# A fused attention and two-layer kernel: half of the low parts of U leave VectorE, and the second pair's attention moves some slots on

## The chip, the cores and the metric

One Trainium2 core runs the whole program. The metric is the device time of one execution in microseconds (us). The engines are named as the profile names them: PE (TensorE, matmuls), PEld (its weight loads), DVE (VectorE), ACT (ScalarE), POOL (GpSimd) and SP, whose queue issues the DMAs.

## The reference, cut to what matters

```
a   = softmax of phi over the sequence                # per batch and head, 32 memories
k_m = a^T k ; v_m = a^T v                             # 32 x 64 each
att = softmax(q k_m^T / 8) over the memories          # 576 x 32 per head
x   = (att v_m) for 4 batches, 8 heads, 576 tokens    # 2304 x 512
h   = max(x w1, x w2, x w3)                           # 2304 x 768
y   = h w_out                                         # 2304 x 512
out = softplus(y w_in2) w_out2                        # 2304 x 2048, then 2304 x 512
```

The weights arrive as 64-bit floating-point numbers. Products are taken with each operand split into a high part (fp32r) and a low part (the rest), so every product is three matmuls: high x high, low x high, high x low.

## The kernel before

The four batches are worked in two pairs (576 x 2 = 1152 tokens each). A unit u is half of the heads of one batch; units 0 to 3 are the first pair, 4 to 7 the second. The stages are:

1. `PLAN`, a list written by hand: attention of units 0 to 3, the conversion of the weights of the first column blocks, the first U matrices and the first four `m1` steps.
2. `phase_a(0)`: 20 slots. In each slot stands one `m1`, and with some of them the U matrices of the next block. There are six column blocks i = 0 to 5 of 128 columns of w1, w2, w3.
3. `phase_o(0)`: 18 slots of `m1out` (the product with w_out).
4. `phase_a(1)` and `phase_o(1)`: the same for the second pair.
5. The last product pair (`m2in`, `m2out`, lines 850 and 882), which takes over half of the time and which the change doesn't touch.

Since attention is linear in v_m, the kernel doesn't form x. It forms U = v_m w (per block i and head pair p, `u_mm`), and multiplies U by the attention weights (`m1`). `u_mm` fills one PSUM bank `X` (128 x 384) by three matmuls (lines 561 to 563). The two halves of its partitions belong to the two batches of the pair. For each half, ACT writes the high part `uh` out of PSUM (line 568) and DVE subtracts it from `X` and writes the low part `ul` (line 572). The bank is free when the four instructions are done. `m1` uses three PSUM banks (18 matmuls at line 589), which ACT (line 593, `mt`) and DVE (lines 594, 596) empty into `h`. Six banks named `psm` serve both.

A weight tile is converted by the class `Conv`: ACT (line 259), DVE (lines 262 and 263), ACT for the high part (line 229), POOL for the low part (line 237). The tile `cg` in between has two buffers for all weights.

Next to its slots, a phase has a list `bg` of work that is put into the program behind slot n. Its numbers stand in the dictionary `C`: `att` (second pair: maxima of phi, exponentials, nothing, the products with k and v, their transposition), `wo` (conversion of w_out, three steps for each of six tiles), `load5` (loads of unit 5) and the literal 3 in `bg[3]` (loads of unit 4). Slots of 20 and over run behind `phase_a(0)`'s last. `C["hl"]` names the engine of the low part of h in `hsplit`.

The slots set the order of the program text. The order on each engine is laid down afterwards by the framework's planner, from times that it simulates (`schedule_with_timeline_sim=True`): an instruction that it holds to be ready may run ahead of others that stand before it. Tiles of one name share its buffers, and wait for each other there.

Of the kernel before, what the change touches and what calls it, by code (L numbers as in the profile page):

```python
# [9 lines left out]
F32 = mybir.dt.float32  # L10
F32R = mybir.dt.float32r
I32 = mybir.dt.int32
AF = mybir.ActivationFunctionType
ALU = mybir.AluOpType
# [117 lines left out]
]  # L132

C = {
    'load5': 5,
    'att': [[9, 9, 10, 11, 11], [10, 12, 12, 13, 13], [13, 13, 15, 15, 15], [15, 18, 19, 21, 21]],
    'wo': [[4, 5, 5], [6, 7, 7], [11, 11, 14], [11, 13, 17], [21, 22, 24], [23, 23, 23]],
    'scs': [[4, 4, 4, 4, 5, 6], [5, 5, 5, 6, 6, 7], [6, 6, 6, 7, 10, 10], [8, 11, 12, 13, 14, 18]],
    's1': ['pool', 'pool', 'pool', 'dve'],
    's2': ['dve', 'pool', 'pool', 'dve'],  # L140
# [2 lines left out]
    'w7': [4, 8, 9, 6],  # L143
    'w8l': 17,
    'wo_off': {(4, 0): 1, (5, 3): 0, (5, 1): -1, (3, 3): -1, (3, 0): 0, (4, 1): -2, (3, 2): 0, (5, 0): -1, (3, 1): 1, (5, 2): -2, (4, 3): 0, (4, 2): 0},
    'hl': ['dve'] + ['pool'] * 16 + ['dve'],
    'us0': 1,
    'us1': 0,
    'qpe': (0, 1, 2, 3),
# [3 lines left out]
def fused_kernel(ctx: ExitStack, tc: tile.TileContext, q, k, v, phi, w1, w2, w3, w_out, m_in, m_out, out):  # L153
# [7 lines left out]
    nc = tc.nc  # L161
# [4 lines left out]
    P = 128  # L166
    SCALE = 1.0 / float(D) ** 0.5
    NJ = FF1 // P
# [16 lines left out]
    def pool(stack, name, side=None, space=None):  # L185
        kw = {"side": side} if side else {"space": space}
        return stack.enter_context(tc.tile_pool(name=name, bufs=1, **kw))
# [6 lines left out]
    a_p = pool(a1_s, "a1", side="right")  # L194
# [7 lines left out]
    def psm():  # L202
        return ps_p.tile([P, 512], F32, tag="m", name="psm", bufs=6)
# [17 lines left out]
    for h in range(4):  # L221
        a = slice(32 * h, 32 * h + 32)
# [61 lines left out]
    def new_vT(pp):  # L284
        vT[pp] = tuple(a_p.tile([P, H, 64], F32R, tag=f"v{x}", name=f"v{x}", bufs=2) for x in "hl")

    def load_phi(u):
        b, g = units[u]
        hs = slice(4 * g, 4 * g + 4)
        if u == 2:  # L290
            ph = t_p.tile([P, 4, R4 + 1, M], F32, tag="qr", name="ph")
        else:
            ph = t_p.tile([P, 4, R4 + 1, M], F32, tag="ph", name="ph", bufs=2)
        dma(out=ph[:, :, 0:R4, :].rearrange("p h r m -> p h (r m)"),
                          in_=phi[b, hs, 0:R4 * P, :].rearrange("h (p r) m -> p h (r m)", r=R4))
        dma(out=ph[0:SREM, :, R4, :], in_=phi[b, hs, R4 * P:S, :].rearrange("h p m -> p h m"))
        nc.gpsimd.memset(ph[SREM:P, :, R4, :], 0.0)
        U[u]["ph"] = ph

    def load_x(u, i):  # L300
        b, g = units[u]
        hs = slice(4 * g, 4 * g + 4)
        src = (k, v)[i]
        if u in (2, 3):
            x = h_p.tile([P, 4, R4, D], F32, tag=f"h{2 * u - 1 - i}", name="kvm")
        else:
            x = t_p.tile([P, 4, R4, D], F32, tag=f"x{i}", name="kvm", bufs=2)
        if u in (2, 3):
            xr = wo_p.tile([SREM, 4, D], F32, tag=f"woh{2 * u - 2 + i}", name="kvr")
        else:  # L310
            xr = t_p.tile([SREM, 4, D], F32, tag=f"xr{i}", name="kvr", bufs=2)
        dma(out=x.rearrange("p h r d -> p h (r d)"),
                          in_=src[b, hs, 0:R4 * P, :].rearrange("h (p r) d -> p h (r d)", r=R4))
        dma(out=xr, in_=src[b, hs, R4 * P:S, :].rearrange("h p d -> p h d"))
        U[u]["x", i] = (x, xr)
# [234 lines left out]
    def u_mm(i, p, bls=(0, 1)):  # L550
        vh, vl = vT[i // NJ]
        vh_p = vh[:, 2 * p:2 * p + 2, :].rearrange("p a c -> p (a c)")
        vl_p = vl[:, 2 * p:2 * p + 2, :].rearrange("p a c -> p (a c)")
        hi, lo = wj_t[i, p]
        assert CK["w", 5 if i == 6 else i, p].done
        for bl in bls:
            for g in range(2):
                assert ("v", 2 * (i // NJ) + bl, g) in CK
            CK["u", i, p, bl] = 1
        X = psm()[:, 0:3 * P]  # L560
        nc.tensor.matmul(X, vh_p, hi, start=True, stop=False)
        nc.tensor.matmul(X, vl_p, hi, start=False, stop=False)
        nc.tensor.matmul(X, vh_p, lo, start=False, stop=True)
        halves = [(p % 2) ^ bl for bl in bls]
        for half in halves:
            uh, ul = Uj[i][(p % 2) ^ half]
            a = slice(64 * half, 64 * half + 64)
            nc.scalar.activation(out=uh[a, p // 2, :], in_=X[a], func=AF.Copy)
        for half in halves:
            uh, ul = Uj[i][(p % 2) ^ half]  # L570
            a = slice(64 * half, 64 * half + 64)
            nc.vector.tensor_tensor(out=ul[a, p // 2, :], in0=X[a], in1=uh[a, p // 2, :], op=ALU.subtract)  # L572

    def m1(i, bl, c):
        pp, j = i // NJ, jof(i)
# [78 lines left out]
    def phase_a(pp, bg, us):  # L654
# [16 lines left out]
        def u2(i, a):  # L671
            if a == 0:
                u_new(i)
            u_mm(i, a)
            u_mm(i, a + 1)
# [39 lines left out]
    for x in vT[0]:  # L715
        for s in range(4):
            nc.gpsimd.memset(x[:, 2 * s + 1 - s % 2].bitcast(F32), 0.0)
    STEPS = dict(ph=load_phi, ld=load_x, q=load_q, mx=att_max, ex=att_exp, ax=att_x, tr=att_tr, qT=att_q,
                 sc=att_sc, s0=att_sm0, s1=att_sm1, s2=att_sm2, fin=att_fin, wl=w_load, ca=conv_a, cb=conv_b,
                 un=u_new, u=u_mm, m1=m1)  # L720
    for st in PLAN:
        f = STEPS[st[0]]
# [7 lines left out]
    bg = defaultdict(list)  # L730
    def load_u(u):
        load_phi(u)
        load_x(u, 1)
        load_x(u, 0)

    bg[3].append(lambda: (new_vT(1), load_u(4)))
    bg[C["load5"]].append(lambda: load_u(5))
    for n in range(4):
        u = 4 + n
# [13 lines left out]
    bg = defaultdict(list)  # L753
# [63 lines left out]
    bg = defaultdict(list)  # L817
# [8 lines left out]
    bg = defaultdict(list)  # L826
# [75 lines left out]
    bg = defaultdict(list)  # L902
# [46 lines left out]
```

## Time and profile before

| | us |
|---|---|
| median of 3 runs (739.6 to 744.3) | 743.75 |
| profiled execution | 744.26 |
| its span in the trace | 742.5 |
| PE busy | 704.9 (95%) |
| DVE busy | 435.3 (59%) |
| ACT busy | 318.7 (43%) |
| POOL busy | 273.1 (37%) |

The span is what the trace shows of the profiled execution; 1.8 us lie around it. A busy share of PE is not PE at its peak: matmuls are pipelined, and a stretch of 100% can hold slower and faster streams.

### The profile page before, as it was taken

Reading aid. Unit: us, or ns where it says so; the run is one execution under the profiler, and the core shown is the slowest. Engines: PE = TensorE matmul, PEld = TensorE weight load, DVE = VectorE, ACT = ScalarE, POOL = GpSimd, SP = SyncE. Lnnn points to the kernel's source line nnn. Section 1 sums busy time; section 2 is a strip of 40 time slices with the busy share of each in tenths; the row PEclk is TensorE's granted clock in tenths of the full one; section 3 lists DMA queues with packets and bytes.
Section 4 is the critical chain, followed back from the end, with each engine's and each line's share of the span. In section 5 each row is a group of like instructions: output and inputs, shape, how many; then the busy total and the mean of one; then the engine's idle time right before and its main releaser. Section 6 shows DMA issues by size and latency. Waiting matters only on the chain. (4 is left out here: it accounts for less than half of the span.)

```text
span 742.5 us, 12551 instructions
## 1 busy us (share of the span) xinstructions
PE 704.9 (95%) x4784; PEld 630.4 (85%) x4784; DVE 435.3 (59%) x816; ACT 318.7 (43%) x662; POOL 273.1 (37%) x268
## 2 busy tenths in 40 slices
PE   4888899999979999989999999999999999999997
PEld 3656698999969999978998988989888989898896
DVE  5479888846969984683333486333794334433342
ACT  2466567644566753552333453222442223222221
POOL 2134333335765324662222353222642223322221
PEclk9989999999999999999999999999999999999999
DMA  8997633413224400440000132000231000011112
GB/s 240 256 305 216 199 100 116 123 56 100 80 71 135 129 2 30 141 143 28 0 1 1 29 113 86 1 0 1 84 115 29 1 1 0 1 43 43 42 43 85
DMA packets 55195, 59.26 MB, mean 80 GB/s; under 512 B 10080, under 2 KB 49504, under 8 KB 55136
## 3 DMA queue, kind: packets, MB, share of 16 engines
q1 hardware_dynamic: 55136, 58.47, 26.6%
q8 instruction: 37, 0.61, 0.4%
q14 instruction: 22, 0.18, 0.1%
HBM read 53.74 MB, written 4.72 MB: 79 GB/s over the span
## 5 line engine op out<-in xcount | busy, mean ns | idle before, releaser
L237 POOL TENSOR_TENSOR gl<-m,gh 128x384 fp32r<-128x384 f32 x96 | 100.6, 1049 | 255.1 <-ACT gh L229 238.1
L856 DVE TENSOR_SCALAR e<-pst 128x384 int32<-128x384 int32 x96 | 53.2, 555 | 135.8 <-PE pst L850 135.7
L858 ACT ACTIVATE L<-e 128x384 f32<-128x384 f32 x96 | 50.3, 524 | 186.1 <-DVE e L856 186.0
L882 PE MATMUL acc<-oh,gh 128*128 128x512 f32 x288 | 113.9, 395 | 0.4 <-ACT gh L229 0.4
L882 PE MATMUL acc<-ol,gh 128*128 128x512 f32 x288 | 113.5, 394 | 0.0
L850 PE MATMUL pst<-yb,ih 128*128 128x384 f32 x384 | 102.1, 336 | 0.0
L589 PE MATMUL psm<-ah,uh 128*128 128x288 f32 x288 | 87.2, 307 | 6.1 <-ACT ya L229 2.1
L860 DVE SCALAR_TENSOR_TENSOR m<-pst,L 128x384 f32<-128x384 f32 x96 | 53.4, 556 | 55.9 <-ACT L L858 55.9
L589 PE MATMUL psm<-al,uh 128*128 128x288 f32 x288 | 85.5, 298 | 0.0
L589 PE MATMUL psm<-ah,ul 128*128 128x288 f32 x288 | 83.8, 298 | 0.6 <-DVE ul L572 0.6
L882 PE MATMUL acc<-oh,gl 128*128 128x512 f32 x288 | 82.7, 394 | 0.0
L229 ACT ACTIVATE gh<-m 128x384 fp32r<-128x384 f32 x96 | 50.0, 523 | 63.1 <-DVE m L860 60.2
L237 POOL TENSOR_TENSOR wl<-cg,wh 128x384 fp32r<-128x384 f32 x44 | 46.3, 1058 | 74.9 <-ACT wh L229 61.0
L850 PEld LDWEIGHTS pst<-yb,ih 128*128 128x128 f32 x384 | 70.0, 188 | 3.4 <-DVE m L860 0.7
L262 DVE TENSOR_SCALAR cg<-cg 128x384 int32<-128x384 int32 (+2 forms) x88 | 46.8, 531 | 37.3 <-ACT cg L259 19.8
L850 PE MATMUL pst<-y0h,ih 128*128 128x384 f32 x192 | 65.5, 341 | 2.7 <-DVE m L860 2.6
L850 PE MATMUL pst<-y0l,ih 128*128 128x384 f32 x192 | 65.1, 339 | 0.0
L850 PE MATMUL pst<-y0h,il 128*128 128x384 f32 x192 | 65.0, 339 | 0.0
L850 PE MATMUL pst<-yb,il 128*128 128x384 f32 x192 | 64.4, 335 | 0.0
L589 PEld LDWEIGHTS psm<-ah,uh 128*128 128x128 f32 x288 | 53.9, 188 | 11.1 <-ACT ya L229 2.3
L882 PEld LDWEIGHTS acc<-oh,gl 128*128 128x128 f32 x288 | 53.6, 187 | 11.4
L882 PEld LDWEIGHTS acc<-oh,gh 128*128 128x128 f32 x288 | 54.1, 188 | 10.6 <-ACT gh L229 0.9
(134 smaller groups left out, 1419.4 us busy)
## 6 DMA issues: line engine op xcount, KB each, us to landing
wraw<-in_moe_w_dram SPq DMA_DIRECT2D x66, 256.0 KB, 3.7
raw<-in_moe_w_in_dram SPq DMA_DIRECT2D x16, 512.0 KB, 3.8
raw<-in_moe_w_out_dram SPq DMA_DIRECT2D x16, 512.0 KB, 3.7
out_dram<-o SPq DMA_DIRECT2D x18, 256.0 KB, 2.1
kvm<-in_v_dram SPq DMA_DIRECT2D x8, 512.0 KB, 6.2
kvm<-in_k_dram SPq DMA_DIRECT2D x8, 512.0 KB, 7.1
wor<-in_moe_w_out_dram SPq DMA_DIRECT2D x6, 512.0 KB, 4.4
qr<-in_q_dram SPq DMA_DIRECT2D x4, 576.0 KB, 4.1
```

What stands on the lines that cost most here:

```text
L229: nc.scalar.activation(out=dst, in_=src, func=AF.Copy)
L237: e.tensor_tensor(out=dst, in0=src, in1=hi, op=ALU.subtract)
L262: nc.vector.tensor_scalar(out=gi, in0=gi, scalar1=3, scalar2=None, op0=ALU.logical_shift_left)
L589: nc.tensor.matmul(x, l[:, t, ws], r[:, cs], start=(n == 0), stop=(n == 5))
L850: nc.tensor.matmul(hx, l[:, ds], r[:, cs], start=(n == 0), stop=(n == 3 * ND - 1))
L856: nc.vector.tensor_scalar(out=e.bitcast(I32), in0=hx.bitcast(I32), scalar1=0x7FFFFFFF, scalar2=None, op0=ALU.bitwise_and)
L858: nc.scalar.activation(out=L, in_=e, func=AF.Softplus, scale=-1.0)
L860: nc.vector.scalar_tensor_tensor(out=m, in0=hx, scalar=0.0, in1=L, op0=ALU.max, op1=ALU.add)
L882: nc.tensor.matmul(acc[0][t], l[:, t * P:(t + 1) * P], r, **kw)
```

## The change

Three things are changed. First, `att`, `wo`, `load5` and the loads of unit 4 stand later in `phase_a(0)`: unit 4's loads behind slot 7 instead of 3, unit 5's behind 9 instead of 5, unit 4's attention from slot 11 instead of 9, and the conversion of w_out spread evenly over slots 10 to 21 instead of 4 to 24. Second, for the blocks of the first pair (`i < NJ`), the low part of the upper half of the partitions is no longer made by DVE out of PSUM: ACT copies that half of `X` to a new tile `xc` in SBUF (one buffer), and POOL subtracts `uh` from it. The lower half and the second pair stay as they were. Third, the very first low part of h goes to POOL instead of DVE, in both `phase_o`.

```diff
-    'load5': 5,
-    'att': [[9, 9, 10, 11, 11], [10, 12, 12, 13, 13], [13, 13, 15, 15, 15], [15, 18, 19, 21, 21]],
-    'wo': [[4, 5, 5], [6, 7, 7], [11, 11, 14], [11, 13, 17], [21, 22, 24], [23, 23, 23]],
+    'load5': 9,
+    'att': [[11, 11, 12, 12, 13], [13, 13, 14, 14, 15], [15, 15, 16, 16, 17], [17, 18, 19, 20, 21]],
+    'wo': [[10, 11, 11], [12, 13, 13], [14, 15, 15], [16, 17, 17], [18, 19, 19], [20, 21, 21]],
...
-    'hl': ['dve'] + ['pool'] * 16 + ['dve'],
+    'hl': ['pool'] * 17 + ['dve'],
...
-            nc.vector.tensor_tensor(out=ul[a, p // 2, :], in0=X[a], in1=uh[a, p // 2, :], op=ALU.subtract)
+            if half and i < NJ:
+                xc = a_p.tile([P, 3 * P], F32, tag="xc", name="xc", bufs=1)
+                nc.scalar.activation(out=xc[a], in_=X[a], func=AF.Copy)
+                nc.gpsimd.tensor_tensor(out=ul[a, p // 2, :], in0=xc[a], in1=uh[a, p // 2, :], op=ALU.subtract)
+            else:
+                nc.vector.tensor_tensor(out=ul[a, p // 2, :], in0=X[a], in1=uh[a, p // 2, :], op=ALU.subtract)
...
-    bg[3].append(lambda: (new_vT(1), load_u(4)))
+    bg[7].append(lambda: (new_vT(1), load_u(4)))
     bg[C["load5"]].append(lambda: load_u(5))
```

## Rows read from the trace of the kernel before

**Rows 1.** Busy time by engine in stretches of the span (us, with instruction counts).
```profile
core 0: us, PE busy (x) PEld busy (x) DVE busy (x) ACT busy (x) POOL busy (x), PEclk, DMA share, GB/s
45.00:95.00 50.00, 45.02 (x558) 34.98 (x559) 45.65 (x100) 32.00 (x73) 18.09 (x17) 0.90 0.80 229
95.00:145.00 50.00, 50.00 (x443) 45.64 (x442) 42.37 (x98) 36.02 (x87) 17.44 (x19) 1.00 0.36 112
160.00:205.00 45.00, 44.79 (x257) 41.69 (x256) 34.54 (x59) 22.23 (x48) 28.69 (x27) 1.00 0.26 80
205.00:230.00 25.00, 19.68 (x117) 18.14 (x116) 18.07 (x32) 16.63 (x37) 18.68 (x17) 0.93 0.27 85
```

**Rows 2.** Waits of PE from 45 to 95 us: total, times, longest.
```profile
PE psm L398 <- ACT kvd L387: 2.5, 1, 2.5
PE psm L469 <- ACT qT L229: 1.9, 2, 1.5
PE psm L589 <- DVE ul L572: 1.2, 2, 0.6
PE psm L589 <- ACT ah L513: 1.1, 1, 1.1
```

**Rows 3.** PE in order of time: the step that starts the slots of phase_a(0).
```profile
89.49 1.15 PE L589 MATMUL psm<-ah,uh 128*128 128x288 f32 x6 [1.15 <-ACT ah L513]
```

**Rows 4.** DVE in order of time, 74 to 81 us: start, length, line, tiles.
```profile
74.27 2.17 DVE L572 TENSOR_TENSOR ul<-psm,uh 64x384 fp32r<-64x384 f32 x4
...
77.36 1.11 DVE L572 TENSOR_TENSOR ul<-psm,uh 64x384 fp32r<-64x384 f32 x2
78.51 0.97 DVE L237 TENSOR_TENSOR hlo<-h,hh 128x384 fp32r<-128x384 f32 x1
79.51 1.14 DVE L572 TENSOR_TENSOR ul<-psm,uh 64x384 fp32r<-64x384 f32 x2
80.58 0.73 DVE L498 TENSOR_REDUCE ssm<-sT 128x18 f32<-128x576 f32 x1
```

**Rows 5.** ACT in order of time, 71 to 77 us.
```profile
71.06 1.85 ACT L568 ACTIVATE uh<-psm 64x384 fp32r<-64x384 f32 x4
...
73.28 0.96 ACT L568 ACTIVATE uh<-psm 64x384 fp32r<-64x384 f32 x2
...
74.82 0.99 ACT L568 ACTIVATE uh<-psm 64x384 fp32r<-64x384 f32 x2
75.72 0.67 ACT L492 ACTIVATE sT<-sT 128x576 f32<-128x576 f32 x1
```

**Rows 6.** POOL at 71 us, and all its low parts of weights (ns: shortest, median, longest).
```profile
71.18 1.34 POOL L491 TENSOR_TENSOR sT<-sT,smx 128x576 f32<-128x576 f32 x1
...
L237 POOL TENSOR_TENSOR wl<-cg,wh x44: 997/1012/1521, 14.0 to 268.6; 128x384 fp32r<-128x384 f32 x44
```

**Rows 7.** Two DVE operations over the whole span (ns: shortest, median, longest).
```profile
L572 DVE TENSOR_TENSOR ul<-psm,uh x96: 482/552/562, 51.1 to 275.2; 64x384 fp32r<-64x384 f32 x96
L263 DVE SCALAR_TENSOR_TENSOR cg<-wraw,cg x44: 509/552/1401, 12.6 to 267.4; 128x384 int32<-128x384 int32 x44
```

**Rows 8.** SP's queue in order of time: the first load of q of unit 4.
```profile
50.22 0.79 SPq L200 DMA_DIRECT2D qr<-in_q_dram  x1
```

**Rows 9.** DVE by line, 45 to 95 us: busy us, mean ns, idle before.
```profile
L572 DVE TENSOR_TENSOR ul<-psm,uh 64x384 fp32r<-64x384 f32 x16 | 8.7, 552 | 0.2
...
L341 DVE TENSOR_TENSOR m<-ph 128x256 f32<-128x256 f32 x4 | 2.2, 552 | 0.2 <-DMA ph<-in_phi_dram 0.2
```

**Rows 10.** ACT by line, 95 to 145 us.
```profile
L568 ACT ACTIVATE uh<-psm 64x384 fp32r<-64x384 f32 x32 | 15.2, 483 | 1.4 <-PE psm L563 1.0
...
L259 ACT ACTIVATE cg<-wor 128x256 f32<-128x256 f32 x8 | 3.4, 436 | 5.6 <-DMA wor<-in_moe_w_out_dram 3.2 <-POOL wl L237 2.4
```

**Rows 11.** Waits of PE from 205 to 230 us.
```profile
PE psm L589 <- ACT ya L229: 2.1, 1, 2.1
PE psm L561 <- DVE ul L572: 1.4, 1, 1.4
```

## The prediction

> **What bounds the kernel now.** Read the busy time by stretches first, then PE's waits in the stretches that the change touches, and then the order on the engines ahead of the waits that remain.
>
> The change works between about 45 us (the first U matrices) and 230 us (the second pair's first slots). In between there are three kinds of stretch [rows 1]. From 45 to 95 us PE is busy 45.02 of 50 us, so 5.0 us are open, and DVE is busy 45.65 of 50, nearly all of the time. From 95 to 145 us PE is busy for all 50.00 us, and from 160 to 205 for 44.79 of 45: there the other engines have slack (DVE 42.37 of 50 and ACT 36.02 of 50 in the first of the two), and nothing that is made faster on them can shorten the time. From 205 to 230 us PE is busy 19.68 of 25; 5.3 us are open at the turn from the first pair to the second.
>
> So a gain can come from two places only, 5.0 us at the start and 5.3 us at the turn. At the start PE's waits are 2.5 us for a scaled k or v on ACT, 1.9 for a transposed q on ACT, 1.2 for the low parts of U on DVE and 1.1 for the attention weights `ah` [rows 2]. The last is the one that counts most, because it is the gate of the slots: the wait just ahead of 89.49 us is for the `ah` of unit 3, without which no `m1` of the pair's second batch can start [rows 3]. Ahead of it PE fills its time with products of the second pair, which have to be done anyway.
>
> What made unit 3 late is read off DVE and ACT. Its exponentials at 75.72 us stood behind eight copies `uh` of block 1 on ACT [rows 5], although GpSimd had given the input at 71.18 + 1.34 = 72.52 us [rows 6]. The sums of these exponentials (line 498) then started at 80.58 us instead of 76.4 (75.72 + 0.67), because eight low parts `ul` (2.17 + 1.11 + 1.14 us) and one `hlo` (0.97) were in front of them on DVE in the same seven microseconds [rows 4]. That is the queue from which the change takes instructions.
>
> **Low parts of U.** There are 6 blocks x 4 head pairs = 24 `u_mm` of the first pair, each with one upper half. So DVE loses 24 of its 48 `ul` at 0.552 us [rows 7], 13.2 us; ACT gets 24 copies and POOL 24 subtractions. The nearest row for the copy is the `uh` copy, the same shape out of PSUM: 483 ns [rows 10]. For the subtraction it is the low part of a weight, the same 384 elements a partition on twice the partitions: 997 to 1521 ns, median 1012 [rows 6]. From below, half of the partitions could cost half of that, 0.5 us; I take 1.0, since the shape along the free axis is the same, and keep 0.5 for the range.
>
> Of the 24, eight lie in the start (16 `ul` there, blocks 0 and 1 [rows 9]), 16 in the slots. In the slots PE waits for nothing, so the 16 x 0.552 = 8.8 us taken from DVE are worth nothing there. At the start the path is unit 3's. In front of line 498 DVE loses four `ul` (4 x 0.552 = 2.2 us) and the `hlo` (0.97, the third part of the change): 3.2 us, so that the sums could start at 77.4. But ACT gets four more copies in front of the exponentials: four copies in a row take 1.85 us [rows 5], so each further one adds (1.85 - 0.48) / 3 = 0.46, and four add 1.8 us, so that these end at 76.4 + 1.8 = 78.2. The later of the two counts: 78.2 against 80.58, a gain of 2.4 us.
>
> From that goes what GpSimd takes back from DVE. Beside GpSimd some operations of DVE with both inputs in SBUF are held up: line 263 takes 509 to 1401 ns, median 552 [rows 7], while `ul`, which reads PSUM, stays within 482 to 562. Five more POOL operations of 1.0 us fall in these seven microseconds (four subtractions and `hlo`). If none holds anything up the price is 0; if each holds one up by the full 1401 - 552 = 849 ns it is 4.2 us, and the gain is gone with 1.8 us to spare. The nearest row in kind is the median, which is at the undisturbed end; I take 0.12 us for each, 0.6 in all. The sum for the start is -2.4 + 0.6 = -1.8 us, with the bounds -5.0 (all of PE's open time) and +1.8.
>
> The Trainium skill speaks against this part (Perfetto Trace Analysis, Optimizing Scalar/DVE Operations): since GpSimd and DVE share an SBUF read port, moving work from the one to the other may not help. By that rule the start would give nothing back, and the sum would be 0. The trace agrees for line 263 (up to 1401 ns), but not for the operation that is moved, whose longest is 562 ns.
>
> In block 0 (48 to 58 us) the same edit puts four copies, 1.8 us, on ACT ahead of the q transposes of unit 2, for which PE waited 1.5 us [rows 2]. ACT idles behind them, so unit 2 can be up to 1.8 us later; unit 3's exponentials had 75.72 - 72.52 = 3.2 us of waiting on ACT, which cover that. I take 0. Without that cover it costs 1.8 us.
>
> **The slots of the second pair's attention and of w_out.** By name the work moves two slots and more. But the planner doesn't keep to the slots where an engine is idle in its own times: q of unit 4, which stands in the program behind all of `phase_a(0)`, is issued at 50.22 us [rows 8], and the maxima of phi (line 341) of all four units of the second pair, slots 9 to 15, run before 95 us [rows 9]. Moving them to slots 11 to 17 leaves them ready at the same times; nothing with a higher place in the program is ready instead. So SP's queue keeps its loads early (the load of w_out may come behind those of unit 5, not in front), and I cost the move at nothing. The cover for that is PE's 50.00 of 50 [rows 1]. For the conversion of w_out the cover is the same: its eight steps on ACT between 95 and 145 us (3.4 us [rows 10]) move to later slots, and `m1out` takes the tiles one by one, in order, over 45 us. If the cover is gone, the bound is from below the 5.0 us open at the start, and from above the 5.3 us of the turn once more.
>
> **What else a new wait holds up.** `xc` has one buffer, so a copy waits for the subtraction before, and everything behind it on ACT waits with it: `mt` and `uh` copies, which empty PSUM banks. A `u_mm` takes ACT 2 x 0.48 + 0.46 = 1.4 us and POOL 1.0 us, so alone the buffer is free in time. In the slots ACT goes from 36.02 to 36.02 + 16 x 0.46 = 43.4 of 50 us, 87%, less what w_out's later slots take away. I cost it at 0 there.
>
> **The sum.** The profiled execution took 744.26 us (a span of 742.5 and 1.8 around it). Less 1.8 us that is 742.5. It stands 0.5 us above the median of the runs, so against the median of 743.75 the change gives 741.95: 742 us. With the bounds of the start, -5.0 to +1.8, and block 0's 1.8 on top, this case spans 739 to 747.
>
> **The rivals.**
> *ScalarE becomes the bound (slower).* The planner puts another POOL operation, 1.0 us, between two subtractions. The next copy `xc` then stands on ACT for 1.0 us, in order, and `mt` behind it; `m1` can't get its three banks and PE stops. ACT's slack in the slots is 50 - 43.4 = 6.6 us. It decides from the seventh of the 16 copies that stands for a full operation; when all do, 16 x 1.0 - 6.6 = 9.4 us go to PE: 753, without the gain at the start. For it: ACT would be the most loaded engine beside PE. Against it: POOL is busy only 17.44 of 50 us there [rows 1], and 33 with the 16 subtractions. When half of the excess reaches PE it is 748.
> *The turn gets worse or better (either sign).* There PE waits 2.1 us for banks that ACT empties late and 1.4 for `ul` [rows 11]. If a later second pair comes to the turn with as much again to do, the 5.3 us open there double: 749. Against it: the last of unit 7's steps stays at slot 21.
> *The slots do work as written (faster).* If the second pair's 2.2 us of maxima and the rest of it leave the start, and the turn loses its waits too, all open time goes: 5.0 + 5.3 = 10.3 us, 733. Against it: rows 8, where the planner goes past twenty slots.
> *GpSimd takes back what DVE gives (no change).* Each of the five POOL operations ahead of unit 3's sums holds DVE up by 2.4 / 5 = 0.48 us, a little over half of the 0.85 that line 263 shows at its worst [rows 7]; the start gives nothing, and the time is 744. Against it: that line's median is only 0.04 us over its shortest. The skill's rule above leads to the same time.
>
> **How the numbers follow.** Differences under 1% (7.4 us) can hardly be told from no change here: three runs span 739.6 to 744.3. The forecast has 0.41, no change 0.14, ScalarE as bound 0.22, a worse turn 0.10, the faster case 0.13. Faster by over 1% means under 736.3: nearly all of the faster case and a little of the forecast, 0.14. Slower by over 1% means over 751.2: half of ScalarE's case, half of the turn's and some of a reordering that I can't see, 0.20. Within 1% is left with 0.66. The range goes from the fastest case's end, 733, to ScalarE's worst, 753; the forecast's own range is 739 to 747.
>
> **What would show it.** In the profile after, DVE should be 10 to 14 us less busy, ACT 11 and POOL 24 us more (12 if half of the partitions cost half). The first `m1` behind unit 3's `ah` should start near 87.7 us instead of 89.49, and everything up to 205 us should be earlier by the same. The maxima of the second pair should still run before 95 us. PE should show no waits from 95 to 145 us; waits there for `mt` would speak for ScalarE as the bound. The prediction is wrong if the planner's new order moves the turn at 205 us by more than the start gives, in either direction.

## The result, and the profile after

| | before | after |
|---|---|---|
| median (4 runs each) | 743.58 us | 752.0 us |
| range of the runs | 739.6 to 744.3 | 751.5 to 754.7 |
| profiled execution | 744.26 us | 754.73 us |
| span, mean granted clock | 742.5 us, 0.988 | 753.0 us, 0.979 |
| PE busy | 704.9 us | 708.5 us |
| DVE, ACT, POOL busy | 435.3, 318.7, 273.1 | 436.2, 330.4, 303.1 |

The ratio is 1.013, 95% interval 1.0104 to 1.0156: the changed kernel is slower by 9.7 us (1.3% of 743). The forecast was 742.

Busy time by stretches of the changed kernel, first the four of [rows 1], then the start in pieces of 5 us (columns as there):

```profile
45.00:95.00 50.00, 40.64 (x449) 31.30 (x449) 39.42 (x82) 33.23 (x73) 26.42 (x25) 0.83 0.75 216
95.00:145.00 50.00, 50.00 (x600) 42.45 (x600) 34.59 (x73) 36.86 (x85) 26.20 (x25) 1.00 0.30 92
160.00:205.00 45.00, 40.19 (x228) 37.51 (x227) 39.02 (x63) 20.60 (x46) 29.84 (x29) 0.96 0.28 88
205.00:230.00 25.00, 20.29 (x97) 19.36 (x96) 18.43 (x24) 14.43 (x33) 16.43 (x15) 0.86 0.35 108
75.00:80.00 5.00, 3.09 (x30) 2.24 (x29) 3.35 (x9) 4.87 (x12) 4.15 (x5) 0.97 0.01 2
80.00:85.00 5.00, 2.65 (x10) 2.06 (x10) 5.00 (x10) 3.55 (x9) 3.75 (x4) 0.50 0.34 107
85.00:90.00 5.00, 4.46 (x48) 3.92 (x47) 4.31 (x8) 2.61 (x6) 3.02 (x4) 0.84 0.59 169
```

The same pieces of the kernel before:

```profile
75.00:80.00 5.00, 3.85 (x37) 3.03 (x29) 4.89 (x11) 3.07 (x6) 1.20 (x2) 1.00 0.84 250
80.00:85.00 5.00, 4.88 (x62) 4.07 (x62) 4.97 (x15) 3.34 (x9) 1.00 (x1) 1.00 0.51 134
85.00:90.00 5.00, 3.85 (x113) 3.04 (x113) 4.87 (x12) 2.09 (x6) 3.72 (x3) 1.00 0.63 179
```

The start was to gain 1.8 us. Instead PE is busy 40.64 of 50 us from 45 to 95 us, 4.4 us less than in [rows 1], and from 80 to 85 us it is busy 2.65 of 5 us at half clock, with 10 matmuls where the kernel before ran 62. From 160 to 205 us PE has lost another 4.6 us. In between it is busy all the time, as forecast.

PE's waits from 45 to 95 us in the changed kernel (total, times, longest), beside [rows 2]:

```profile
PE psm L398 <- ACT kvd L387: 3.1, 1, 3.1
PE psm L469 <- ACT qT L229: 2.6, 1, 2.6
PE psm L594 <- ACT xc L574: 1.9, 1, 1.9
PE pst L350 <- DVE md L349: 1.4, 1, 1.4
PE psm L449 <- ACT xc L574: 1.1, 1, 1.1
PE psm L594 <- POOL ul L575: 1.0, 1, 1.0
```

`ah` of unit 3, the wait on which the prediction rested [rows 3], is gone. Two new names stand in its place: `xc` on ACT and `ul` on POOL (line 594 is `m1`, 574 the copy, 575 the subtraction). ACT and then POOL in order of time show where these two stood:

```profile
76.16 0.67 ACT L492 ACTIVATE sT<-sT 128x576 f32<-128x576 f32 x1
78.84 0.47 ACT L574 ACTIVATE xc<-psm 64x384 f32<-64x384 f32 x1
80.86 0.68 ACT L513 ACTIVATE ah<-aT 128x576 fp32r<-128x576 f32 x1
81.56 0.49 ACT L574 ACTIVATE xc<-psm 64x384 f32<-64x384 f32 x1
83.47 0.49 ACT L574 ACTIVATE xc<-psm 64x384 f32<-64x384 f32 x1 [0.34 <-POOL ul L575]
87.55 0.49 ACT L574 ACTIVATE xc<-psm 64x384 f32<-64x384 f32 x1
```

```profile
79.96 0.99 POOL L575 TENSOR_TENSOR ul<-xc,uh 64x384 fp32r<-64x384 f32 x1
82.12 1.31 POOL L575 TENSOR_TENSOR ul<-xc,uh 64x384 fp32r<-64x384 f32 x1 [1.17 <-ACT xc L574]
83.51 2.38 POOL L237 TENSOR_TENSOR wl<-cg,wh 128x384 fp32r<-128x384 f32 x2
85.97 1.00 POOL L575 TENSOR_TENSOR ul<-xc,uh 64x384 fp32r<-64x384 f32 x1
88.11 0.99 POOL L575 TENSOR_TENSOR ul<-xc,uh 64x384 fp32r<-64x384 f32 x1 [1.00 <-ACT xc L574]
```

Unit 3 did come earlier: its sums (line 498) start at 76.87 us against 80.58 [rows 4]. But block 1's four copies lie spread over 78.84 to 88.04 us, between other work of ACT, and the last low part of block 1 is finished on POOL at 89.10 us. In the kernel before DVE had finished all of them by 80.65 [rows 4]. The `m1` steps on block 1 need these low parts, and the PSUM banks that the copies hold. The gate moved from unit 3's `ah` to block 1's U. The fifth `h`, the first that needs unit 3's `ah`, was to come 1.8 us earlier; it is done at 97.5 us against 94.7 before.

DVE is not relieved either. Its rows by shape, changed kernel (busy us, mean ns), then the kernel before:

```profile
L577 DVE TENSOR_TENSOR ul<-psm,uh 64x384 fp32r<-64x384 f32 x72 | 39.0, 549 | 9.3 <-ACT uh L568 4.6 <-ACT xc L574 3.2 <-PE psm L594 0.9
L263 DVE SCALAR_TENSOR_TENSOR cg<-wraw,cg 128x384 int32<-128x384 int32 x44 | 34.5, 791 | 0.7
L263 DVE SCALAR_TENSOR_TENSOR cg<-wor,cg 128x256 int32<-128x256 int32 x12 | 10.0, 845 | 0.0
```

```profile
L572 DVE TENSOR_TENSOR ul<-psm,uh 64x384 fp32r<-64x384 f32 x96 | 52.2, 552 | 8.6 <-ACT uh L568 7.4
L263 DVE SCALAR_TENSOR_TENSOR cg<-wraw,cg 128x384 int32<-128x384 int32 x44 | 29.4, 673 | 0.5
L263 DVE SCALAR_TENSOR_TENSOR cg<-wor,cg 128x256 int32<-128x256 int32 x12 | 6.4, 544 | 0.0
```

`ul` went down by 13.2 us, as forecast; line 263, the same 56 instructions, went up by 8.7. The trace shows what these 8.7 us go with. Of the 44 operations on `wraw`, those that had POOL at work for half of their length or more were 13 before and 21 after, with medians of 1111 and 1243 ns; the others took a median of 549 and 552 ns.

### The profile page after: what moved, and what is told of

Read it like the earlier page. It is cut to its first block, busy times and chain, and to the rows that moved or that the text cites. A ratio compares the mean times of both kernels' runs of the same rounds, so it can differ in the third digit from the quotient of the medians.

```text
span 753.0 us, 12579 instructions
## 1 busy us (share of the span) xinstructions
PE 708.5 (94%) x4784; PEld 634.0 (84%) x4784; DVE 436.2 (58%) x790; ACT 330.4 (44%) x686; POOL 303.1 (40%) x294
## 5 line engine op out<-in xcount | busy, mean ns | idle before, releaser
L594 PE MATMUL psm<-ah,uh 128*128 128x288 f32 x288 | 89.0, 310 | 6.5 <-ACT mt L598 2.8
L262 DVE TENSOR_SCALAR cg<-cg 128x384 int32<-128x384 int32 (+2 forms) x88 | 48.8, 559 | 35.8 <-ACT cg L259 18.6
L237 POOL TENSOR_TENSOR wl<-cg,wh 128x384 fp32r<-128x384 f32 x44 | 48.0, 1098 | 43.7 <-ACT wh L229 41.0
L887 PEld LDWEIGHTS acc<-oh,gh 128*128 128x128 f32 x288 | 53.9, 187 | 10.5 <-ACT gh L229 0.9
```

Source lines behind the costliest of these rows:

```text
L237: e.tensor_tensor(out=dst, in0=src, in1=hi, op=ALU.subtract)
L262: nc.vector.tensor_scalar(out=gi, in0=gi, scalar1=3, scalar2=None, op0=ALU.logical_shift_left)
L594: nc.tensor.matmul(x, l[:, t, ws], r[:, cs], start=(n == 0), stop=(n == 5))
L887: nc.tensor.matmul(acc[0][t], l[:, t * P:(t + 1) * P], r, **kw)
```

## The experiments

The difference is the ratio to the kernel before on the same chip, less one, times 743 us. "Copies" are the `xc` copy on ACT and its subtraction on POOL.

| kernel | ratio, 95% interval | difference |
|---|---|---|
| the change | 1.013, 1.0104 to 1.0156 | +9.7 |
| e1: without the copies | 1.002, 0.9997 to 1.0042 | +1.5 |
| e2: copies alone, all blocks | 1.015, 1.0123 to 1.0177 | +11.1 |
| e3: the change, old w_out slots | 1.0167, 1.014 to 1.0194 | +12.4 |
| e4: the change, two buffers | 1.0113, 1.0083 to 1.0144 | +8.4 |
| e5: copies in blocks 0, 1 | 1.0055, 1.0034 to 1.0076 | +4.1 |
| e6: copies in blocks 2 to 5 | 0.9955, 0.9934 to 0.9976 | -3.3 |
| e7: copies, DVE subtracts | 1.0125, 1.0086 to 1.0164 | +9.3 |
| e8: copies that nobody reads | 1.0088, 1.006 to 1.0117 | +6.5 |
| e9: the change, copies in 2 to 5 | 1.0071, 1.0044 to 1.0098 | +5.3 |
| e10: copies in block 0 | 0.9991, 0.9972 to 1.0009 | -0.7 |
| e11: copies in block 1 | 1.0059, 1.0038 to 1.0081 | +4.4 |
| e12: copies in 0 and 2 to 5 | 1.0014, 0.9993 to 1.0034 | +1.0 |
| e13: copies in 1 to 5 | 1.0135, 1.0103 to 1.0167 | +10.0 |
| e15: e11 with filled stop | 1.001, 0.999 to 1.0029 | +0.7 |
| e16: the filling alone | 1.0012, 0.9988 to 1.0035 | +0.9 |
| e17: the change, filled stop | 1.0063, 1.0046 to 1.0081 | +4.7 |
| e18: e13, all `ya` on ACT | 1.0094, 1.0074 to 1.0113 | +7.0 |

### Which of the three parts

e1 is the changed kernel with line 572 as before (the slots and the engine of `h` stay changed); e2 is the kernel before with the copies alone; e3 is the changed kernel with the old `wo`.

```diff
 e1 (to the changed kernel)
-            if half and i < NJ:
...
+            nc.vector.tensor_tensor(out=ul[a, p // 2, :], in0=X[a], in1=uh[a, p // 2, :], op=ALU.subtract)
 e3 (to the changed kernel)
-    'wo': [[10, 11, 11], [12, 13, 13], [14, 15, 15], [16, 17, 17], [18, 19, 19], [20, 21, 21]],
+    'wo': [[4, 5, 5], [6, 7, 7], [11, 11, 14], [11, 13, 17], [21, 22, 24], [23, 23, 23]],
```

> The changed kernel without the copy: all low parts of U made by VectorE again, the new slots and the GpSimd low part of h kept. Theory 1 (the copies through the single xc buffer are the cost: ScalarE's copy waits for GpSimd's subtraction, GpSimd has other work in between, the low parts and the PSUM banks come late): the loss goes, 741 to 746 us. Theory 2 (the slots are the cost: the conversion of w_out inside the last slots makes ScalarE wait for w_out's loads ahead of the mt copies): it stays at 749 to 753. Theory 3 (the planner's new order, no single part): anything, and the parts do not add up to +8.4 us.

> The kernel before with the copy and GpSimd subtraction alone. Theory 1: nearly the whole loss, 749 to 754 us, with the last low part of block 1 near 89 us instead of 80.6. Theory 2: 741 to 746. Theory 3: anything, not the complement of the run without the copy.

> The changed kernel with w_out's conversion at its old slots. Theory 1: 750 to 754 us, nothing won. Theory 2: 744 to 748, and no wait of PE for mt of over 1 us between 145 and 185 us (2.8 us in the changed kernel). Theory 3: anything.

Measured 743.57, 753.53 and 754.75 us. Without the copies no loss can be told from nothing; with them alone the whole loss is there. That the slots cost nothing by themselves was right, and w_out's slots are not the cause: with the old ones (e3) the time is no better, and 0.75 us above my range.

### The buffer, the engine, or the copies themselves

e4 gives `xc` two buffers (paid for with one of the two of `md`); in e7 DVE subtracts from `xc`; in e8 DVE subtracts from PSUM as before, and ACT makes 24 copies that nobody reads.

```diff
 e4 (to the changed kernel)
-        md = t_p.tile([P, P], F32, tag="md", name="md", bufs=2)
+        md = t_p.tile([P, P], F32, tag="md", name="md", bufs=1)
-                xc = a_p.tile([P, 3 * P], F32, tag="xc", name="xc", bufs=1)
+                xc = t_p.tile([P, 3 * P], F32, tag="xc", name="xc", bufs=2)
 e7 (to e2)
-                nc.gpsimd.tensor_tensor(out=ul[a, p // 2, :], in0=xc[a], in1=uh[a, p // 2, :], op=ALU.subtract)
+                nc.vector.tensor_tensor(out=ul[a, p // 2, :], in0=xc[a], in1=uh[a, p // 2, :], op=ALU.subtract)
 e8, in its place
+                nc.vector.tensor_tensor(out=ul[a, p // 2, :], in0=X[a], in1=uh[a, p // 2, :], op=ALU.subtract)
```

> The changed kernel with two xc buffers (in another pool; the small diagonal tile md goes from two buffers to one to make room). Theory 1: the waits of ScalarE's copy for GpSimd's subtraction (5.0 us in all) fall under 2 us, and a third to a half of the loss goes, 746 to 750 us; the rest is GpSimd's queue. Theory 2: 750 to 754, no gain. Theory 3: anything.

> The kernel before with ScalarE's copy into xc for all 24, the subtraction out of xc by VectorE instead of GpSimd. If GpSimd (its 1.0 us and its queue) makes the low parts late: 742 to 746 us. If ScalarE's 24 further copies (11.7 us) are the cost whoever subtracts: 749 to 754.

> The kernel before with ScalarE's 24 copies added and read by nobody; VectorE subtracts out of PSUM as before. It adds ScalarE's time and keeps the bank, without a wait for a subtraction. If ScalarE's load is the cost: 747 to 753 us; if the dependence on GpSimd is: 742 to 746.

Measured 750.98, 752.54 and 749.35 us. In e4 ACT's waits for POOL's subtraction fall from 5.0 us to none, but the time falls by 1.3 us of 9.7 only, which the intervals can't tell from nothing; I had expected 746 to 750. POOL isn't needed for the loss (e7), and 24 more readings of the banks by ACT, with no new engine in the chain, already cost 6.5 (e8). The start of e8 shows a loss as well: PE is busy 41.68 of 50 us from 45 to 95 us there, at a clock of 0.77. So most of the price is in the copies. Whether it is ACT's time or the bank held longer isn't separated by these runs.

### At the start or in the slots

```diff
 e5 (to e2)
-            if half and i < NJ:
+            if half and i < 2:
 e6 (to e2), e9 (to the changed kernel)
-            if half and i < NJ:
+            if half and 2 <= i < NJ:
```

> The kernel before with the copy and GpSimd subtraction in blocks 0 and 1 alone (8 of 24, those in the hand-written part). Theory 1a (the cost lies at the gate of the slots: block 1's low parts come late): 5 to 8 us slower than before, 748 to 751 us. Theory 1b (the cost lies in the slots): 741 to 745.

> The kernel before with the copy and GpSimd subtraction in blocks 2 to 5 alone (16 of 24). Theory 1a: 743 to 747 us, some 3 us at most. Theory 1b: 749 to 753. If the two places add up, this and the run with blocks 0 and 1 together lose the 10.7 us of the run with all 24.

> The changed kernel with xc in blocks 2 to 5 alone (the slots); blocks 0 and 1 get their low parts from VectorE again. Theory (the loss is made in the start, blocks 0 and 1, and xc in the slots is worth 3.3 us as it was alone): the new slots and the first low part of h cost nothing, so about 740 us, 3 to 4 below the kernel before, and about 12 below the changed one. Rival (the slots' xc gains only together with the old slot list, since the gain is one of order): 742 to 746.

Measured 746.87, 740.28 and 747.18 us. Blocks 0 and 1 alone lose 4.1 us. The 16 copies in the slots gain 3.3 with the old slot lists, and lose with the new ones. None of the ranges held: e5 lies between its two theories, e6 below both of its own, e9 above both. Stretches of e6, then of e9:

```profile
95.00:165.00 70.00, 62.17 (x615) 54.80 (x614) 56.81 (x114) 50.28 (x118) 37.50 (x39) 0.98 0.36 113
205.00:230.00 25.00, 24.14 (x158) 23.82 (x157) 18.94 (x34) 17.00 (x40) 17.02 (x17) 1.00 0.28 85
```

```profile
95.00:165.00 70.00, 66.81 (x730) 58.12 (x729) 43.71 (x102) 46.95 (x112) 34.06 (x36) 1.00 0.35 112
205.00:230.00 25.00, 19.73 (x112) 18.33 (x111) 18.12 (x32) 14.38 (x32) 18.03 (x17) 0.93 0.31 97
```

In both, PE is open in the slots, 7.8 us (e6) and 3.2 us (e9) of 70, where it was open 0.0 before; its longest waits there are for `mt`, 3.0 and 1.3 us. So copies in the slots were not free. e6 gets it back at the turn, where PE is busy 24.14 of 25 us instead of 19.68 [rows 1] and the clock stays at 1.00: the second pair's attention is worked while `m1` stands (its four `ah` start at 172.5 to 188.5 us against 185.0 to 211.1 before), and little is left to wait for. e9 gets nothing back (19.73; its `ah` run from 188.5 to 214.5). So the stretches read e6's gain as one of order at the turn, not of DVE's relief; no run separates the two. Early attention alone doesn't bring it: in the changed kernel the four `ah` start at 173.6 to 198.4 us, nearly as early as in e6, and PE is busy 20.29 of 25 us. e6 is the fastest kernel of the study; its interval, 0.9934 to 0.9976, lies wholly under 1.

### Which block of the start, and whether prices add

```diff
 e10, e11, e12 and e13 (to e2), in this order
-            if half and i < NJ:
+            if half and i == 0:
+            if half and i == 1:
+            if half and i < NJ and i != 1:
+            if half and i < NJ and i != 0:
```

> The kernel before with xc in block 0 alone (4 copies, 4 subtractions). Theory (the loss comes from block 1's copies, behind which unit 3's exponentials and the low parts of the slots' second step stand): within 1 us of the kernel before. Rival (each of the eight copies of the start costs alike): +2 us. Third (block 0's copies delay unit 2's q, the cover that the prediction named): +1.8 us or more, with a longer wait of PE for qT between 45 and 95 us.

> The kernel before with xc in block 1 alone. Theory (block 1's copies are the cost): +3 to +5 us, the m1 of block 1, first half, late as with both blocks (start near 87 us instead of 78), PE waiting for xc on ACT. Rival (alike): +2 us. Third (block 0): 0.

> The kernel before with xc in every block of the first pair but block 1 (20 copies instead of 24). Theory (block 1 makes the loss, and also what turns the slots' gain of 3.3 us into a loss of 10 when all are together): 740 to 742. Rival (no block is special; the planner's new order with any copies at the start and in the slots loses): 748 to 752.

> The kernel before with xc in blocks 1 to 5 (20 copies, all but block 0's). Theory (block 0's copies cost nothing, and block 1's together with the slots' make the loss of 10 us): 751 to 754. Rival (prices simply add: +4.7 and -3.3): 744 to 745.

Measured 741.9, 747.39, 743.59 and 752.36 us. Block 0's copies cost nothing, block 1's 4.4. The theory's ranges hold but for e12, 1.6 us above its own, and for the start of `m1` in e11, which I expected near 87 us: it starts on time and stops on its way. Prices don't add: block 1 costs 4.4 alone, but 13.3 on top of e6 (e13), and block 0 costs 4.3 on top of e6 (e12) and nothing alone. In e11, PE in order of time:

```profile
75.02 0.32 PE L375 MATMUL pst<-kvr,et 64*32 64x64 f32 x8
77.55 0.61 PE L594 MATMUL psm<-ah,uh 128*128 128x288 f32 x1 [2.21 <-ACT xc L574]
77.96 0.44 PE L594 MATMUL psm<-al,uh 128*128 128x288 f32 x1
...
86.40 0.44 PE L594 MATMUL psm<-ah,ul 128*128 128x288 f32 x1
86.64 0.37 PE L594 MATMUL psm<-ah,uh 128*128 128x288 f32 x1
86.85 0.30 PE L594 MATMUL psm<-al,uh 128*128 128x288 f32 x1
```

The second bank of the `m1` on block 1 is the one that the first `xc` copy read last, so PE stands 2.2 us at 75.3. Behind the stop each matmul of 288 columns takes 0.44 us instead of 0.30 (their starts lie 0.24 us apart instead of 0.13), until 86.6: the granted clock of e11 is 0.66 from 75 to 80 us, 0.50 to 85 and 0.82 to 90, where the kernel before shows 1.00 three times (it has falls of its own ahead of 60 us and behind 90, 0.90 over the whole start [rows 1]). Of these 15 us, 10.2 are at the lower of the two levels, 1.2 GHz ((0.34 + 0.50 + 0.18) x 5 x 2); 3.4 of them lie ahead of 80 us, more than the 2.4 us left behind the stop, so the clock fell while PE still stood. The Trainium skill (TensorE: Matmul & The Clock Gate, What's actually happening) states that how busy PE was sets which level it gets, and this trace agrees. From 60 to 95 us PE is open 5.3 us in e11 and 2.8 before, and the clock is 0.85 against 0.95, which is 3.5 us of full speed: 2.5 us more open time and 3.5 us of clock together are more than the 4.4 us by which the kernel is slower.

### The stop, and the clock behind it

e15 puts 16 matmuls into the first bank of that `m1` step, ahead of its own, which overwrite them. They stand in PE's order where the stop was. e16 puts them into the kernel before, e17 into the changed kernel.

```diff
 e15 (to e11), e16 (to the kernel before), e17 (to the changed kernel)
             ws = slice(w * P, (w + 1) * P)
+            if (i, bl, c, w) == (1, 0, 0, 0):
+                for _ in range(16):
+                    nc.tensor.matmul(x, uh[:, 0, ws], attn[2 * pp + bl, 0][0][:, cs], start=True, stop=True)
             n = 0
```

> The kernel with xc in block 1 alone, and 16 further matmuls (128x288, 0.13 us each, 2.1 us together) in the first PSUM bank of the m1 step on block 1, first half, ahead of its own products, which overwrite them: PE works where it stood 2.2 us for xc. Theory (half of block 1's price is the fall of PE's clock to half speed behind that stop, not the stop): granted clock at 1.00 from 75 to 90 us, and 3 us less than the 747.4 of xc in block 1 alone, so 744 to 745, although PE has 2.1 us more to do. Rival (the price is the stop and the later low parts alone): 747 to 749.5.

> The kernel before with the same 16 further matmuls: what the filling itself costs. Theory and rival alike: they run where PE was busy, so up to +2.1 us (745), less what of it falls into the 1.2 us that PE is open there.

> The changed kernel with the 16 further matmuls (2.1 us) in the first bank of the m1 step on block 1, first half. Theory (the price at the start is as with block 1 alone, where they brought 4 us): 747 to 749. Rival (the changed kernel loses most at its turn, which comes after and has stops of its own, so what the start regains is lost there again): 751 to 754.

Measured 743.32, 743.43 and 747.98 us. With 2.1 us more to do, e11 and the changed kernel both come out 4 us earlier; in the kernel before the filling costs 0.9 us, with an interval of -0.9 to +2.6 that excludes neither 0 nor its own 2.1. e15's PE, then its stretches:

```profile
73.53 2.38 PE L592 MATMUL psm<-ah,uh 128*128 128x288 f32 x16
...
77.71 0.40 PE L597 MATMUL psm<-ah,uh 128*128 128x288 f32 x1
```

```profile
75.00:80.00 5.00, 3.84 (x85) 2.99 (x88) 4.08 (x12) 4.58 (x11) 2.39 (x4) 1.00 0.57 180
80.00:85.00 5.00, 4.72 (x135) 3.46 (x128) 4.56 (x9) 3.39 (x9) 4.36 (x5) 0.59 1.02 272
85.00:90.00 5.00, 5.00 (x40) 4.24 (x40) 4.68 (x9) 1.61 (x5) 2.33 (x2) 0.73 1.03 293
```

The stop for `xc` is gone and the clock stays at 1.00 to 80 us, but then it falls all the same, for 6.8 us instead of 10.2. So the time went the theory's way (0.7 us below its range), but not wholly for its reason: the shorter stretch at half clock is worth 3.4 / 2 = 1.7 us at most, and the rest is that PE's waits from 60 to 95 us fall from 5.3 us in e11 to 1.8; behind 84 us PE's order is another one. What is shown is that ACT's and POOL's work as such is not the price of block 1, since in e15 the same copies and subtractions cost nothing that can be told (+0.7). How the 4.4 us divide among the stops, half clock and the planner's new order isn't shown.

In e17 PE is busy 44.13 of 50 us from 45 to 95 us, 3.5 more than in the changed kernel, and 2.1 of these are the filling. From 160 to 230 us it is busy 63.35 us instead of 60.48, and the clock is 1.00 instead of 0.93. So a good part of what the filling returned there came at the turn, and it isn't the price of the one stop.

### The turn

e13 shows where block 1 and the slots lose together. DVE at the turn, then PE, in order of time:

```profile
201.36 2.26 DVE L262 TENSOR_SCALAR cg<-cg 128x384 int32<-128x384 int32 x2 [1.39 <-ACT cg L259]
203.54 2.64 DVE L263 SCALAR_TENSOR_TENSOR cg<-wraw,cg 128x384 int32<-128x384 int32 x2
206.11 2.39 DVE L262 TENSOR_SCALAR cg<-cg 128x512 int32<-128x512 int32 x2
208.42 2.88 DVE L263 SCALAR_TENSOR_TENSOR cg<-raw,cg 128x512 int32<-128x512 int32 x2
211.22 0.55 DVE L233 COPY ya<-psm 128x384 f32<-128x384 f32 x1
```

```profile
211.82 0.69 PE L635 MATMUL psm<-hh,woh 128*128 128x384 f32 x1 [4.12 <-DVE ya L233]
```

The copy `ya` that frees a bank of `m1out` stands behind 10 us of weight conversions; PE stops for 4.1 us, and the clock is 0.57 from 210 to 215 us. In e6 the 512-wide conversions are done by 199.1 us, and `ya` follows at 205.82. e18 gives all these copies to ACT; PE's order stays all but the same.

```diff
 e18 (to e13)
-                    cast("dve" if dm % 2 else "act", y1[pp, dm][:, cs], yps[0][dm])
+                    cast("act", y1[pp, dm][:, cs], yps[0][dm])
```

> The kernel with xc in blocks 1 to 5 (752.4 us), in which the first pair's copies ya, which empty the four banks of m1out, are all made by ScalarE instead of half by VectorE. In that kernel PE stood 4.1 us behind a ya that stood on VectorE behind 10 us of weight conversions (lines 262, 263) at 201 to 211 us, and the clock fell to 0.57 behind it. Theory (the part of the loss that block 1 and the slots make only together lies in this stop at the turn, and in the clock behind it): 4 to 7 us less, 745 to 748. Rival (the open time at the turn returns in another place, as ScalarE empties the banks no sooner): 750 to 753.

Measured 750.09 us, 2.3 less than e13 and at the lower end of the rival's range: the theory fell. PE's longest wait of e18 from 200 to 235 us:

```profile
PE psm L635 <- DVE ul L577: 3.4, 1, 3.4
```

The banks then wait for `ul` behind the same conversions, so the open time did return in another place, as the rival said. The stop belongs to these conversions being early in DVE's order, not to `ya`.

The changed kernel loses at its turn too. From 160 to 230 us PE is open 9.5 us, where the kernel before is open 5.5 and e13 8.1, and the clock is 0.93 against 0.98 and 0.95. Its longest waits from 160 to 235 us:

```profile
PE psm L594 <- ACT mt L598: 2.8, 2, 2.5
PE psm L635 <- ACT ya L229: 2.4, 1, 2.4
PE psm L561 <- DVE ul L577: 2.0, 1, 2.0
```

The second pair's attention is done earlier there than before (first `ah` at 173.6 us against 185.0), and still nothing is gained. What each of these stops costs isn't shown.

## Why the prediction was wrong, point by point

**The step that failed** is the pricing of block 1's four copies: "four copies in a row take 1.85 us, so each further one adds 0.46, and four add 1.8 us", and "the path is unit 3's". They were priced as a delay of unit 3's exponentials, at the end of a row of `uh` copies. In fact ACT's order put the exponentials first (76.16) and the copies behind and between other work up to 88.04 us. The copies didn't delay unit 3, whose sums came 3.7 us earlier instead of the forecast 2.4; they delayed what the prediction didn't follow, the bank `X` and the low parts of block 1. It thought of banks only by way of the one buffer, in the slots, and at 0. The start was to gain 2.4 us less 0.6; measured for block 1 alone it is +4.4 (e11), outside the bound of +1.8.

**A size missing from the sum** is the clock. No step had a price for PE at half speed behind a new stop. The mean clock of the profiled executions (the changed kernel's is the slowest of its four) says how large it can be: (1 - 0.979) x 753.0 = 15.8 us of full speed not granted, against (1 - 0.988) x 742.5 = 8.9. That is up to 6.9 of the 10.5 us between the spans, an upper bound, since PE also waits in some of that time. Filling one stop returned 4.0 us of the change's loss (e17), though partly at the turn.

**"In the slots PE waits for nothing, so 0" failed too**, with a smaller price: in the changed kernel itself, copies in the slots alone make e9's +5.3 us. That 5.3 and block 1's 4.4 come to 9.7 is no proof, as prices don't add elsewhere. With the old slot lists the turn returns what the slots lose (e6), with the new ones it doesn't (e9); that is a matter of order that no row of before could tell. Why the planner lays e6 out so well, and why block 0 costs 4.3 us only on top of e6, stays open.

**Right** were: the moved slots cost nothing as long as VectorE makes all `ul` (e1: +1.5, interval -0.2 to +3.1); block 0 costs nothing (e10), though by luck in part, as unit 2's `ah` starts 5.8 us later there (75.8 against 70.0) where 1.8 was allowed for; PE is busy 50.00 of 50 from 95 to 145 us; the maxima of the second pair still run before 95 us (the last at 89.44); ACT has 11.7 us more, forecast 11.

**DVE's relief fell**: forecast 10 to 14 us less, measured 0.9 more. Line 263's 8.7 us are most of what came back, line 262 (2.0 us more) and small operations the rest. POOL itself has 30.0 us more, forecast 24: 24 subtractions at a median of 1008 ns are 24.2, the rest are two `hlo` and instructions held up. Here the Trainium skill's rule on moving work between DVE and GpSimd (Perfetto Trace Analysis, Optimizing Scalar/DVE Operations) was the better guide for DVE's total, 435.3 against 436.2 us; the trace of before agreed with it for line 263, and for line 262, which I didn't read. The term was mis-sized: I took 0.12 us for each POOL operation from a median over operations of which most had no POOL beside them, where 8.7 us over 26 new ones are 0.33.

**The rivals.** ScalarE as the bound was given 748 to 753, and 752.0 was measured, but by another mechanism: it rested on copies that stand for POOL because of the one buffer. ACT stood for that 5.0 us in all, a second buffer ended these waits and returned 1.3 us (e4), and without POOL in the chain the copies still cost 6.5 (e8). ACT was busy 36.86 of 50 us from 95 to 145 us, not 43.4. The turn as a place of loss (749) came true in part, in e13 and in the changed kernel, but not from a later second pair, whose attention was done earlier. The slots working as written (733) fell with e1. GpSimd taking back what DVE gives is true of the sums and wasn't needed for the loss (e7).

## What to carry to other kernels

A copy that is added to empty a PSUM bank is one more reader of that bank: follow who waits for the bank and for the value made from the copy, and look for both in the engine's actual order, not beside the instruction that it follows in the program. A new stop of PE can cost more than its length where the clock falls behind it (e11), so a sum made at the start of a kernel needs a line for that. A median hides two kinds of operations: sort them by what runs beside them before pricing one more. Where a planner lays out the order, prices of single edits don't add, and a loss can come back at a later turn or not; test edits alone and together.

## What the runs showed of the hardware that was not expected

Moving 24 subtractions of 0.55 us from DVE (out of PSUM) to POOL (out of SBUF) left DVE's busy time where it was: line 263 on w_out's tiles went from a median of 420 ns to 1024 ns, on the others up to 1668 ns, and operations of one shape fall into two groups, 549 ns and, where POOL was at work for at least half of their time, 1111 ns. In e11 the clock fell within a stop of 2.2 us, and 10.2 us went by at half clock. POOL took 1008 ns for a subtraction on 64 partitions, as for one on 128 [rows 6]: half the partitions cost the same. Two microseconds of matmuls whose result is overwritten returned 4 us in two kernels (e15, e17), where they also changed the planner's order.
